# First loads, squares of the norm, and routing order in a fused attention and two-expert-layer kernel

## The chip, the cores and the metric
The kernel runs on one core of one Trainium2 chip. The core has five engines that each work through their own list of instructions in order: TensorE (PE, matrix products and transposes), VectorE (DVE), ScalarE (ACT), GpSimd (POOL) and SyncE (SP, which here only issues transfers). They wait for each other through semaphores. The metric is the device time of one launch in microseconds; it was 1309.68 us in the median of three runs (1309.29 to 1310.69).

## The reference
Three layers follow on each other for 4608 tokens (8 sequences of 576) of width 512:

```
kv  = einsum('bhsd,bhse->bhde', k, v)           # 8 heads of 64, no softmax
out = einsum('bhsd,bhde->bhse', q, kv)
x   = out / sqrt(mean(out*out, -1) + 1e-6) * g_norm
x   = (silu(x @ w_gate) * (x @ w_val)) @ w_out  # dense, hidden width 1536, weights float64
# routed: 8 experts of hidden width 1024, the best one per token
do  = x @ w_skip > 0                            # others pass unchanged
p   = softmax(x @ gate);  e = argmax(p)
y   = x + p[e] * (relu(x @ w1[e]) @ w2[e])      # where do
```

## The kernel before, in words
The work goes in 12 chunks of 384 tokens. The **attention** of a chunk has four units, one for each pair of heads (`attn_unit`). A unit multiplies k by v into a PSUM tile kvp (L211, only where a new sequence begins), copies its two diagonal blocks of 64 x 64 into kvbd, the first on ScalarE (L213), the second on VectorE (L214), multiplies the queries by kvbd into op (L227), squares op on ScalarE (sq, L233), adds the squares up head by head on VectorE (ms, L235), finishes the mean (L236), raises it to the power -1/2 on GpSimd (y, L238) and multiplies (xn, L240). `make_xT` transposes xn (xtps, L262) and splits it into a rounded part and the rest (L265, L266). Products in float32 are made from such pairs: each product is three matmuls.

The **gated layer** (MoE1) goes over 12 slices f of the hidden width in each chunk: gate and value products gv (L346), silu (L352), their product s (L353), the split into hT (L355 on ScalarE, L254 on GpSimd), and with a delay of one slice the accumulation acc (L367) in three PSUM banks. In chunk 0 the units of chunk 1 run between the slices; in later chunks those of the next chunk. Chunk 0 also turns the weights' 64-bit numbers into pairs: 18 transfers raw (L315, the last as two rawh, L324), and for each of 36 halves a rescale on ScalarE (L284), three bit operations on VectorE (L286, L287, L290), a rounding on ScalarE (L296) and the rest on GpSimd (L254). TensorE can begin a slice when its weights are converted.

The **routed layer** (MoE2) works with a list of tokens by expert. Each chunk's rows of x give nine logits a token, on VectorE (L400) during the next chunk, for the last chunk on TensorE (`logits_pe`: transposes ltp, L411, then matmuls lps, L416). `chunk_route` finds the expert and counts ranks by two small matmuls rp (L446, L447); then GpSimd scatters the rows (L454) into the memory xs, from which `load_xe` (L601) fetches a batch xe. A batch is transposed (xtp, L618) into xU, multiplied by the expert's first weights (hp, L633; hr, L655, in the batch of one tile) and its second (yacc, L721).

The first batch needs no rows of the last chunk. Its products hp and yacc fill TensorE while the last chunk is routed; the second batch needs the rows that this routing scatters.

The order within an engine is set by a scheduler that simulates the program ahead of time and takes what is ready first; `after(ins, to)` (L115) gives it an extra condition, which orders the list and adds no wait. SP's list holds all loads in one order: a load that waits for a buffer holds up those behind it. Tiles come from pools: wp has 18 buffers "w", p2 two of each name (kv, s for sq and s, ms), ps_acc three PSUM banks, ps_gv two, ps_x two, ps_c one.

Of the kernel before, what the change touches and what calls it, by code (L numbers as in the profile page):

```python
# [29 lines left out]
def attention_moe_moe_kernel(  # L30
# [98 lines left out]
    def attn_qt_load(c, pr):
        if c == 0:  # L130

            t = wp.tile([P, T], F32, tag="w", name="qt0")
        else:
            t = p1.tile([P, T + P], F32, tag="qt", name="qt")
# [204 lines left out]
    def moe1_g(c, f):  # L339
# [13 lines left out]
        nc.vector.tensor_tensor(s, ps[1], s, op=ALU.mult)  # L353
# [51 lines left out]
    def logits_pe(c, w9):  # L405
        lp = ps_acc.tile([P, R, P], F32, tag="acc", name="lps")
        for r in range(R):
            st = xrow[c, r]
# [6 lines left out]
            for kk in range(NK):  # L415
                nc.tensor.matmul(  # L416
# [7 lines left out]
    def chunk_route(c):  # L424
        lg = lgt.pop(c)
        wd = wdesc.rearrange("p (o e) -> p o e", o=1).to_broadcast([P, R, E])
        eb = (elast if c == NCH - 1 else ebase).rearrange("p (o e) -> p o e", o=1).to_broadcast([P, R, E])
# [592 lines left out]
```

## Time and profile before

| | |
|---|---|
| median of three runs | 1309.68 us |
| the profiled execution | 1305.69 us |
| its span (first to last instruction) | 1304.0 us |
| TensorE busy | 1266.1 us, 97% |
| VectorE, ScalarE, GpSimd busy | 639.3, 373.5, 510.6 us |
| chain that ended last | PE 85%, DVE 5%, DMA 4%, POOL 3% |
| mean granted TensorE clock | 0.995 |

The span is what the profile's times count; the profiled execution's own time stands beside it. Busy time over the whole span is a mean over stages: in one stage TensorE has no gap, in another it waits for a single load. A wait is named by the instruction that waited, the line, and what came last before it. Idle time of an engine that nobody waits for costs nothing. The granted clock is that of TensorE as a share of its upper level, 2.4 GHz.

### The profile page before, as it was taken

Reading aid. Unit: us, or ns where it says so; the run is one execution under the profiler, and the core shown is the slowest. Engines: PE = TensorE matmul, PEld = TensorE weight load, DVE = VectorE, ACT = ScalarE, POOL = GpSimd, SP = SyncE. Lnnn points to the kernel's source line nnn. Section 1 sums busy time; section 2 is a strip of 40 time slices with the busy share of each in tenths; the row PEclk is TensorE's granted clock in tenths of the full one; section 3 lists DMA queues with packets and bytes.
Section 4 is the critical chain, followed back from the end, with each engine's and each line's share of the span. In section 5 each row is a group of like instructions: output and inputs, shape, how many; then the busy total and the mean of one; then the engine's idle time right before and its main releaser. Section 6 shows DMA issues by size and latency. Waiting matters only on the chain.

```text
span 1304.0 us, 18975 instructions
## 1 busy us (share of the span) xinstructions
PE 1266.1 (97%) x7239; PEld 1180.2 (91%) x7239; DVE 639.3 (49%) x1487; ACT 373.5 (29%) x773; POOL 510.6 (39%) x545
## 2 busy tenths in 40 slices
PE   5998999999999999999999999999999989999997
PEld 5987999999999999999999999999988978899996
DVE  5896817237164371542815418146283243544662
ACT  3664112122121221211212112121122433344441
POOL 4674323233322332223323223223346443566662
PEclk9999999999999999999999999999999999999999
DMA  9663702021120111202102021110121343555631
GB/s 299 234 220 142 229 20 74 25 68 43 39 66 1 44 55 38 73 26 63 37 7 86 8 62 49 31 51 7 51 91 36 131 149 117 170 171 165 218 121 33
DMA packets 43205, 115.68 MB, mean 89 GB/s; under 512 B 8498, under 2 KB 16690, under 8 KB 40928
## 3 DMA queue, kind: packets, MB, share of 16 engines
q1 hardware_dynamic: 31888, 95.78, 22.7%
q0 software_dynamic: 6912, 9.82, 2.2%
q10 hardware_dynamic: 4304, 8.78, 2.1%
q8 instruction: 59, 0.97, 0.3%
q14 instruction: 42, 0.34, 0.1%
HBM read 88.70 MB, written 30.80 MB: 92 GB/s over the span
## 4 chain that ended last, share of the span: by engine, by line
PE 85%; DVE 5%; DMA 4%; POOL 3%; issue 2%; ACT 1%; SPq 0%; DVEq 0%; ACTq 0%; POOLq 0%
PE gv L346 42%; PE acc L367 21%; PE hp L633 7%; PE yacc L721 4%; PE tacc L687 3%; PE kvp L211 3%; PE op L227 2%; DVE dump L400 2%; PE xtps L262 1%; DMA kv<-in_kv_dram 1%; DMA xe<-xs_dram 1%; POOL v L254 1%; DMA raw<-in_w_dram 1%; DVE ex L585 1%; POOL w L254 1%
## 5 line engine op out<-in xcount | busy, mean ns | idle before, releaser
L346 PE MATMUL gv<-xT,w 128*128 128x384 f32 x3456 | 654.7, 339 | 3.8 <-ACT w L296 2.9
L346 PEld LDWEIGHTS gv<-xT,w 128*128 128x128 f32 x3456 | 602.1, 188 | 18.3 <-ACT w L296 4.2
L367 PE MATMUL acc<-w,hT 128*128 128x512 f32 x1296 | 333.3, 397 | 5.0 <-ACT hT L355 4.0
L254 POOL TENSOR_TENSOR hT<-s,hT 128x384 fp32r<-128x384 f32 x144 | 161.6, 1122 | 403.8 <-ACT hT L355 403.3
L367 PEld LDWEIGHTS acc<-w,hT 128*128 128x128 f32 x1296 | 239.3, 188 | 49.3 <-ACT hT L355 5.6
L400 DVE CUSTOM_DVE_ANT_0 dump<-st,w9b 128x512 bf16<-128x512 f32 x297 | 234.4, 789 | 7.0
L353 DVE TENSOR_TENSOR s<-gv,s 128x384 f32<-128x384 f32 x144 | 80.1, 556 | 253.0 <-PE gv L346 186.1
L254 POOL TENSOR_TENSOR v<-rawv,v 128x512 fp32r<-128x512 f32 x102 | 133.6, 1335 | 49.9 <-ACT v L567 49.7
L352 ACT ACTIVATE s<-gv 128x384 f32<-128x384 f32 x144 | 70.6, 490 | 260.4 <-PE gv L346 251.2
L355 ACT ACTIVATE hT<-s 128x384 fp32r<-128x384 f32 x144 | 75.5, 524 | 242.5 <-DVE s L353 241.1
L633 PE MATMUL hp<-xU,v 128*128 128x256 f32 (+7 forms) x768 | 125.8, 308 | 1.6 <-DVE xU L623 1.4
L633 PEld LDWEIGHTS hp<-xU,v 128*128 128x128 f32 x768 | 113.8, 189 | 4.7 <-DVE xU L623 1.7
L238 POOL TENSOR_TENSOR y<-ms,mhalf 128x6 f32<-128x6 f32 x48 | 68.2, 1422 | 109.7 <-DVE ms L236 107.8
L235 DVE TENSOR_REDUCE ms<-sq 128x6 f32<-128x384 f32 x48 | 26.4, 550 | 105.7 <-ACT sq L233 105.7
L567 ACT ACTIVATE v<-rawv 128x512 fp32r<-128x512 f32 x128 | 73.0, 623 | 1.9 <-DMA rawv<-in_v_dram 1.9
L721 PE MATMUL yacc<-v,h2T 128*128 128x512 f32 (+3 forms) x288 | 73.3, 397 | 0.0
L642 DVE SCALAR_TENSOR_TENSOR h2T<-hp,h2T 128x256 fp32r<-128x256 f32 (+7 forms) x64 | 30.5, 479 | 82.3 <-ACT h2T L641 81.1
L721 PEld LDWEIGHTS yacc<-v,h2T 128*128 128x128 f32 (+3 forms) x288 | 50.6, 181 | 11.2
L687 PE MATMUL tacc<-h2T,v 128*128 128x318 f32 (+3 forms) x384 | 58.1, 302 | 2.1 <-ACT h2T L641 2.1
L641 ACT ACTIVATE h2T<-hp 128x256 fp32r<-128x256 f32 (+7 forms) x64 | 27.2, 428 | 104.7 <-PE hp L633 92.1
L254 POOL TENSOR_TENSOR w<-raw,w 128x512 fp32r<-128x512 f32 x34 | 44.7, 1318 | 30.4 <-ACT w L296 29.5
L687 PEld LDWEIGHTS tacc<-h2T,v 128*128 128x128 f32 x384 | 53.8, 189 | 2.9 <-ACT h2T L641 2.8
(131 smaller groups left out, 875.8 us busy)
## 6 DMA issues: line engine op xcount, KB each, us to landing
rawv<-in_v_dram SPq DMA_DIRECT2D x64, 512.0 KB
kv<-in_kv_dram SPq DMA_DIRECT2D x32, 560.0 KB
raw<-in_w_dram SPq DMA_DIRECT2D x17, 1024.0 KB
out_dram<-st SPq DMA_DIRECT2D x36, 256.0 KB
xs_dram<-zrow ACTq DMA_DIRECT2D x8, 781.5 KB
qt<-in_qT_dram SPq DMA_DIRECT2D x32, 192.0 KB
qt<-in_qT_dram SPq DMA_DIRECT2D x32, 96.0 KB
w9b<-in_w_dram ACTq DMA_DIRECT2D x3, 768.0 KB
```

Of the source, the lines that this page charges most:

```text
L238: nc.gpsimd.tensor_tensor(y, ms, mhalf[:, 0:G], op=ALU.pow)
L254: return eng.tensor_tensor(lo, raw, hi.bitcast(F32), op=ALU.subtract)
L346: nc.tensor.matmul(pt, w1t[f][:, wi, i, kk, :], xT[c, kk][:, xi, :], start=(n == 0), stop=(n == 3 * NK - 1))
L352: step["silu"] = nc.scalar.activation(s, ps[0], AF.Silu)
L353: nc.vector.tensor_tensor(s, ps[1], s, op=ALU.mult)
L355: nc.scalar.activation(h[:, 0, :], s, AF.Copy)
L367: nc.tensor.matmul(acc[c, r], hT[c, f][:, hi, r * P:(r + 1) * P], w[:, wi, f % 2, :], start=(f == 0 and n == 0), stop=(f == NF - 1 and n = ...
L400: nc.vector.tensor_tensor_reduce(out=dump, in0=xrow[c, r][:, 0:DM], in1=w9b[m // 3][:, m % 3, :], op0=ALU.mult, op1=ALU.add, scale=1.0, sc ...
L567: after(nc.scalar.activation(w[:, 0, s], raw[:, s], AF.Copy), behind)
L633: nc.tensor.matmul(pt, w[:, wi, kk, cs], xT["m", b, kk][:, xi, :], start=(i == 0), stop=(i == 3 * NK - 1))
L687: nc.tensor.matmul(acc["m", b, d], w[:, wi, f % 2, d * P:(d + 1) * P], h[:, hi, :], start=(f == 0 and n == 0), stop=(f == NF2 - 1 and n == 2),
L721: ins = nc.tensor.matmul(acc["m", b, t][0:q], h[:, hi, t * q:(t + 1) * q], w[:, wi, f % 2, :], start=(f == 0 and n == 0), stop=(f == NF2 - ...
```

## The change
- Loads of k and v go over the flattened rows of the array, 128 rows in one transfer, where 116 were fetched in two (112 and 4). The rows past 116 are not used.
- Chunk 0: k, v and q of a pair share one buffer of wp (kvq). Three are asked for before the first unit. op of pairs 0 to 2 lies in the accumulators' banks, of pair 3 in a bank of gv.
- Chunks 0 and 1: ScalarE copies both blocks of kvbd, and six 64-wide squares that also add up their columns take the place of square and reduction.
- Chunk 1's loads of k, v and q are ordered behind the second weight's conversion. The first and second weights are asked for at other places.
- `chunk_route` ends with rp; the rest is `route_rows`, one slice later and behind s of that slice; `rank_experts` and `early_base` come another slice later.
- First routed batch: hp of slice 1 is ordered behind the second ltp, of slices 2 and 3 behind the last lps, later ones behind rp; yacc of slice 0 behind the last lps, later ones behind rp.

The core of the diff:

```diff
+    kv_rows = kv_d.rearrange("b q p s r c -> (b q p) s r c")
+    def attn_kv_load(c, pr, t, behind=None):
+        if c % 3 != 2:
+            b = 2 * (c // 3) + c % 3
+            row = (b * NPR + pr) * PK
+            n = min(P, B * NPR * PK - row)
+            for lo, hi in spread(n):
+                after(nc.sync.dma_start(t[lo:hi], kv_rows[row + lo:row + hi]), behind)
+            kvt[c, pr] = t
...
+    def attn_load_first(pr):
+        t = wp.tile([P, 2 * NR * P + T], F32, tag="w", name="kvq")
+        attn_kv_load(0, pr, t[:, 0:2 * NR * P].rearrange("p (s r c) -> p s r c", s=2, r=NR))
+        return t[:, 2 * NR * P:]
...
-        step["kv", c, pr] = nc.vector.tensor_copy(bd[D:P, D:P], kvp[D:P, D:P])
+        if c < 2:
+            nc.scalar.activation(bd[D:P, D:P], kvp[D:P, D:P], AF.Copy)
+        else:
+            nc.vector.tensor_copy(bd[D:P, D:P], kvp[D:P, D:P])
...
-            op = gv_tile([P, R, P], "op", True)
+            op = ps_acc.tile([P, R, P], F32, tag="acc", name="op") if pr < 3 else gv_tile([P, R, P], "op", True)
...
-        nc.scalar.activation(sq, opv, AF.Square)
-        nc.vector.tensor_reduce(ms, sq, axis=AX.X, op=ALU.add)
+        if c < 2:
+            for g in range(G):
+                nc.scalar.activation(sq[:, g, :], opv[:, g, :], AF.Square, accum_out=ms[:, g:g + 1])
+        else:
+            nc.scalar.activation(sq, opv, AF.Square)
+            nc.vector.tensor_reduce(ms, sq, axis=AX.X, op=ALU.add)
...
+        step["rp"] = nc.tensor.matmul(rp, onesb, ca[:, 0:R, :], start=False, stop=True)
+        chosen[c] = rp, oh, m1, mk
+    def route_rows(c, behind=None):
+        after(nc.vector.tensor_tensor(oh, rp, eb, op=ALU.add), behind)
...
-    attn_load(0, 1)
+    attn_qt_load(0, 1, attn_load_first(1))
+    qt2 = attn_load_first(2)
     attn_unit(0, 0)
-    for pr in range(1, NPR):
-        if pr + 1 < NPR:
-            attn_load(0, pr + 1)
-        attn_unit(0, pr)
+    attn_unit(0, 1)
     load_w1(0, (step["ms", 0, 0], step["ms", 0, 1]))
+    attn_qt_load(0, 2, qt2)
+    attn_qt_load(0, 3, attn_load_first(3))
+    attn_unit(0, 2)
+    attn_unit(0, 3)
...
-    load_w1(1)
+    load_w1(1, (step["ms", 0, 3], step["xn", 0, 3]))
...
-                    attn_load(c + 1, f // 3)
+                    attn_load(c + 1, f // 3, conv_done.get(1) if c == 0 else None)
...
-                if f == -(-(E + 1) * R // lpf):
+                f0 = -(-(E + 1) * R // lpf)
+                if f == f0:
                     chunk_route(c - 1)
+                if f == f0 + 1:
+                    route_rows(c - 1, step["gv"])
+                if f == f0 + 2:
                     if c == NCH - 2:
-                        rank_experts(c - 1)
+                        rank_experts(c - 1, step["gv"])
...
+    first_h = (None, step["ltp", 1], step["lps", R - 1], step["lps", R - 1], step["rp"])
+    first_y = (step["lps", R - 1], step["rp"])
...
-            moe2_h(b, f)
+            moe2_h(b, f, first_h[min(f, len(first_h) - 1)] if b == 0 else None)
...
-                        moe2_out(b, f - 1, t)
+                        moe2_out(b, f - 1, t, first_y[min(f, 2) - 1] if b == 0 else None)
```

What the lists hold at three places, before and now.

SP at the program's start, before (kv the k and v of a pair, qt0 its queries in chunk 0, qt those of chunk 1, raw a weight; the number is the buffer):
```order
L150 DMA kv_88<-in_kv_dram 112x1280
L150 DMA kv_88<-in_kv_dram 4x1280
L142 DMA qt0_91<-in_qT_dram 128x384
L150 DMA kv_166<-in_kv_dram 112x1280
L150 DMA kv_166<-in_kv_dram 4x1280
L142 DMA qt0_169<-in_qT_dram 128x384
L142 DMA qt0_195<-in_qT_dram 128x384
L142 DMA qt0_221<-in_qT_dram 128x384
L315 DMA raw_265<-in_w1_dram 128x2048
L139 DMA qt_377<-in_qT_dram 128x192
L140 DMA qt_377<-in_qT_dram 128x192
L150 DMA kv_192<-in_kv_dram 112x1280
```
SP there, now (kvq holds k, v and queries of a pair):
```order
L134 DMA kvq_88<-in_kv_dram 128x1280
L149 DMA kvq_88<-in_qT_dram 128x384
L134 DMA kvq_164<-in_kv_dram 128x1280
L149 DMA kvq_164<-in_qT_dram 128x384
L134 DMA kvq_167<-in_kv_dram 128x1280
L333 DMA raw_219<-in_w1_dram 128x2048
L149 DMA kvq_167<-in_qT_dram 128x384
L134 DMA kvq_233<-in_kv_dram 128x1280
L149 DMA kvq_233<-in_qT_dram 128x384
L333 DMA raw_318<-in_w1_dram 128x2048
```
The third pair's k and v moved in front of the first weight and have a buffer of their own; chunk 1's queries are gone from here.

ScalarE from the first unit on, before (kvbd: block copies, raw: rescale, w: rounded half of a weight):
```order
L213 ACTIVATE kvbd_93<-kvp 64x64
L213 ACTIVATE kvbd_97<-kvp 64x64
L233 ACTIVATE sq<-op 128x384 x2
L284 ACTIVATE raw<-raw 128x512 x2
L296 ACTIVATE w_0_267<-raw 128x512
L213 ACTIVATE kvbd_101<-kvp 64x64
L296 ACTIVATE w_0_267<-raw 128x512
```
ScalarE there, now:
```order
L222 ACTIVATE kvbd_91<-kvp 64x64
L224 ACTIVATE kvbd_91<-kvp 64x64
L222 ACTIVATE kvbd_95<-kvp 64x64
L224 ACTIVATE kvbd_95<-kvp 64x64
L250 ACTIVATE sq,ms<-op 128x64 x6
L222 ACTIVATE kvbd_99<-kvp 64x64
L224 ACTIVATE kvbd_99<-kvp 64x64
L250 ACTIVATE sq,ms<-op 128x64 x6
L302 ACTIVATE raw<-raw 128x512 x2
L250 ACTIVATE sq,ms<-op 128x64 x6
L314 ACTIVATE w_0_221<-raw 128x512
```
Twelve narrow squares stand in front of the first rescale of a weight, and eighteen in front of the first rounding.

TensorE where the last chunk is routed, before (two ltp x4 and 23 hp stand in front of these rows; v1 are the expert's first weights, v2 its second):
```order
L416 MATMUL lps_8870<-w9k_8845,lxt0_8876 128x128 x2
L416 MATMUL lps_8870<-w9k_8845,lxt1_8877 128x128 x2
L416 MATMUL lps_8870<-w9k_8845,lxt0_8889 128x128 x2
L416 MATMUL lps_8870<-w9k_8845,lxt1_8890 128x128 x2
L411 MATMUL ltp_8897<-ident_109,st_8866 128x128 x4
L721 MATMUL yacc0_9060<-v2_0_8264,h2T_9037 128x512 x3
L721 MATMUL yacc1_9064<-v2_0_8264,h2T_9037 128x512 x3
L721 MATMUL yacc0_9060<-v2_0_8264,h2T_9057 128x512 x3
L721 MATMUL yacc1_9064<-v2_0_8264,h2T_9057 128x512 x3
L633 MATMUL hp_9123<-xU3_8842,v1_2_8419 128x256
L416 MATMUL lps_8870<-w9k_8845,lxt0_8902 128x128 x2
L416 MATMUL lps_8870<-w9k_8845,lxt1_8903 128x128 x2
```
TensorE there, now:
```order
L429 MATMUL ltp_8881<-ident_107,st_8856 128x128 x4
L660 MATMUL hp_9041<-xU0_8821,v1_0_8210 128x256 x3
L660 MATMUL hp_9041<-xU1_8827,v1_0_8210 128x256 x3
L660 MATMUL hp_9041<-xU2_8833,v1_0_8210 128x256 x3
L660 MATMUL hp_9041<-xU3_8839,v1_0_8210 128x256 x3
L434 MATMUL lps_8867<-w9k_8842,lxt0_8873 128x128 x2
L434 MATMUL lps_8867<-w9k_8842,lxt1_8874 128x128 x2
L429 MATMUL ltp_8894<-ident_107,st_8863 128x128 x4
L434 MATMUL lps_8867<-w9k_8842,lxt0_8886 128x128 x2
L434 MATMUL lps_8867<-w9k_8842,lxt1_8887 128x128 x2
L434 MATMUL lps_8867<-w9k_8842,lxt0_8899 128x128 x2
L434 MATMUL lps_8867<-w9k_8842,lxt1_8900 128x128 x2
```
Between the first two ltp and the last lps 12 hp are left of 24 hp and 12 yacc; 6 yacc and 24 hp now stand between the last lps and rp.

## Rows read from the trace of the kernel before
**Rows 1.** Busy time by stretch: width, engines (instructions), granted clock, DMA share, GB/s
```profile
0.00:10.00 10.00, 3.52 (x15) 3.24 (x16) 0.68 (x3) 1.70 (x3) 3.55 (x45) 1.00 0.81 227
10.00:20.00 10.00, 7.58 (x34) 7.05 (x34) 5.96 (x14) 3.21 (x7) 4.00 (x3) 1.00 1.02 331
20.00:30.00 10.00, 4.86 (x30) 4.65 (x30) 8.83 (x18) 6.26 (x13) 6.03 (x5) 0.94 1.02 310
80.00:120.00 40.00, 34.41 (x170) 28.94 (x170) 31.75 (x51) 21.12 (x38) 25.83 (x21) 1.00 0.44 168
122.00:1025.00 903.00, 900.05 (x4999) 842.52 (x4998) 416.00 (x1096) 205.61 (x419) 296.71 (x319) 1.00 0.17 54
1061.00:1071.00 10.00, 9.06 (x57) 8.42 (x58) 5.23 (x18) 4.73 (x13) 5.22 (x6) 0.83 0.89 324
```

**Rows 2.** Waits of TensorE: for whom, us in total, times, longest
```profile
PE kvp L211 <- DMA kv<-in_kv_dram: 8.9, 4, 6.1
PE xtps L262 <- DVE xn L240: 5.1, 1, 5.1
PE acc L367 <- ACT hT L355: 4.0, 4, 1.6
...
PE xtp L618 <- DMA xe<-xs_dram: 2.8, 1, 2.8
...
PE acc L367 <- POOL hT L254: 1.1, 3, 0.4
...
PE xtp L618 <- DVE xU L623: 0.4, 1, 0.4
```

**Rows 3.** Timeline of TensorE, start: start us, us, instruction, idle before
```profile
16.21 2.47 PE L211 MATMUL kvp<-kv 116*128 116x128 f32 x10 [2.18 <-DMA kv<-in_kv_dram]
18.92 2.47 PE L211 MATMUL kvp<-kv 116*128 116x128 f32 x10 [0.24 <-DMA kv<-in_kv_dram]
...
28.89 0.88 PE L262 MATMUL xtps<-ident,xn 128*128 128x128 f32 x3 [5.14 <-DVE xn L240]
```

**Rows 4.** Tiles kvbd and sq by form: shortest, median, longest ns, first and last start
```profile
L213 ACT ACTIVATE kvbd<-kvp x32: 191/217/218, 8.7 to 859.5; 64x64 f32<-64x64 f32 x32
L214 DVE COPY kvbd<-kvp x32: 227/228/229, 8.9 to 859.8; 64x64 f32<-64x64 f32 x32
...
L233 ACT ACTIVATE sq<-op x48: 467/492/495, 12.8 to 940.2; 128x384 f32<-128x384 f32 x48
L235 DVE TENSOR_REDUCE ms<-sq x48: 541/553/553, 13.3 to 940.8; 128x6 f32<-128x384 f32 x48
```

**Rows 5.** VectorE to 122 us: one conversion step; its wait for squares
```profile
L287 DVE SCALAR_TENSOR_TENSOR cv<-raw,cv 128x512 int32<-128x512 int32 x34 | 23.6, 693 | 1.6
...
DVE ms L235 <- ACT sq L233: 4.9, 3, 2.7
```

**Rows 6.** Timeline of VectorE, end of the conversion
```profile
110.94 0.55 DVE L235 TENSOR_REDUCE ms<-sq 128x6 f32<-128x384 f32 x1 [2.71 <-ACT sq L233]
...
116.51 0.69 DVE L290 SCALAR_TENSOR_TENSOR rawh<-rawh,cv 128x512 int32<-128x512 int32 x1
```

**Rows 7.** Timeline of TensorE, the switch
```profile
1036.52 2.99 PE L633 MATMUL hp<-xU,v 128*128 128x256 f32 x23
...
1041.49 3.02 PE L721 MATMUL yacc<-v,h2T 128*128 128x512 f32 x12
...
1044.47 1.05 PE L416 MATMUL lps<-w9k,lxt 128*128 128x128 f32 x8
...
1051.34 0.19 PE L447 MATMUL rp<-cum,onesb 128*128 128x24 bf16 x1
...
1061.29 0.44 PE L618 MATMUL xtp<-ident,xe 128*128 128x128 f32 x2 [2.77 <-DMA xe<-xs_dram]
...
1065.21 3.67 PE L655 MATMUL hr<-v,xU 128*128 128x256 f32 x24
```

**Rows 8.** Timeline of GpSimd, the switch
```profile
1053.26 1.09 POOL L454 DMA_INDIRECT xs_dram<-st,idx  x1 [4.76 <-DVE cnf L842]
```

More of the change, by code (lines that the diff above doesn't have):

```diff
@@ L123, in after, with attn_qt_load @@
         return ins
+    kv_rows = kv_d.rearrange("b q p s r c -> (b q p) s r c")
[7 more added lines that the diff above has]
+            kvt[c, pr] = t
     def q_at(c, r):
         return r * P + (P if c % 3 == 1 and r > RS else 0)
[L129 to L134, printed above, removed]
+    def attn_qt_load(c, pr, t, behind=None):
         src = qT_d[pr, :, c * T:(c + 1) * T]
@@ L352, in moe1_g @@
         step["silu"] = nc.scalar.activation(s, ps[0], AF.Silu)
-        nc.vector.tensor_tensor(s, ps[1], s, op=ALU.mult)
+        step["gv"] = nc.vector.tensor_tensor(s, ps[1], s, op=ALU.mult)
         h = p2.tile([P, 2, T], F32R, tag="hT", name="hT")
@@ L415, in logits_pe @@
             for kk in range(NK):
-                nc.tensor.matmul(
+                step["lps", r] = nc.tensor.matmul(
                     lp[:, r, :], xt[kk // 2][:, kk % 2, :], w9[:, kk, :], start=(kk == 0), stop=(kk == NK - 1)
@@ L446, in chunk_route @@
         nc.tensor.matmul(rp, trib, mk, start=True, stop=False)
-        nc.tensor.matmul(rp, onesb, ca[:, 0:R, :], start=False, stop=True)
-        nc.vector.tensor_tensor(oh, rp, eb, op=ALU.add)
+        step["rp"] = nc.tensor.matmul(rp, onesb, ca[:, 0:R, :], start=False, stop=True)
+        chosen[c] = rp, oh, m1, mk
+    chosen = {}
+    def route_rows(c, behind=None):
+        rp, oh, m1, mk = chosen.pop(c)
+        eb = (elast if c == NCH - 1 else ebase).rearrange("p (o e) -> p o e", o=1).to_broadcast([P, R, E])
+        after(nc.vector.tensor_tensor(oh, rp, eb, op=ALU.add), behind)
         nc.vector.tensor_tensor(oh, oh, mk, op=ALU.mult)
@@ L480, in count, with by_rank @@
         return cp
-    def by_rank(src, name):
+    def by_rank(src, name, behind=None):
         t = xtp.tile([P, E, E], F32, tag="cmp", name="cmp")
-        nc.vector.tensor_tensor(t, sel, over(src, False), op=ALU.mult)
+        after(nc.vector.tensor_tensor(t, sel, over(src, False), op=ALU.mult), behind)
         o = p2.tile([P, E], F32, tag="rk" + name, name="rk" + name)
@@ L488, in by_rank, with rank_experts @@
         return o
-    def rank_experts(c):
+    def rank_experts(c, behind):
         key = p2.tile([P, E], F32, tag="key", name="key")
-        nc.vector.scalar_tensor_tensor(key, count(c), float(2 * E), wdesc, op0=ALU.mult, op1=ALU.add)
+        after(nc.vector.scalar_tensor_tensor(
+            key, count(c), float(2 * E), wdesc, op0=ALU.mult, op1=ALU.add
+        ), behind)
         t = xtp.tile([P, E, E], F32, tag="cmp", name="cmp")
@@ L512, in load_ranks, with early_base @@
             )
-    def early_base():
-        o = by_rank(count(NCH - 2), "o")
+    def early_base(behind):
+        o = by_rank(count(NCH - 2), "o", behind)
         nc.vector.tensor_scalar(adj, o[:, 0:1], -1.0, float(EARLY), op0=ALU.mult, op1=ALU.add)
@@ L623, in make_xT2, with moe2_h @@
         return nc.vector.tensor_tensor(xt[:, 1, :], tpf, xt[:, 0, :].bitcast(F32), op=ALU.subtract)
-    def moe2_h(b, f):
+    def moe2_h(b, f, behind=None):
         r, _, m, nt = BATCH[b]
@@ L632, in moe2_h @@
             for wi, xi in ((0, 0), (0, 1), (1, 0)):
-                nc.tensor.matmul(
+                ins = nc.tensor.matmul(
                     pt, w[:, wi, kk, cs], xT["m", b, kk][:, xi, :], start=(i == 0), stop=(i == 3 * NK - 1)
                 )
+                if i == 0:
+                    after(ins, behind)
                 i += 1
@@ L833, in attention_moe_moe_kernel @@
     chunk_route(NCH - 1)
+    route_rows(NCH - 1)
     load_xe(1)
```

23 lines of the change are left out of this document (9 added, 14 removed).

## The prediction
> **What bounds the kernel now.** I read the stretches of the span first [rows 1]. From 122 to 1025 us TensorE is busy for 900 of 903 us: eleven of the twelve chunks of the gated feed-forward network have no gaps, and nothing that the change moves there can pay. What TensorE loses lies before 122 us and near the end of the gated network. The waits of TensorE [rows 2] name the places: 8.9 us for four loads of k and v (6.1 of them the first load), 5.1 us for the normalised queries, 4.0 us for the hidden values hT, 2.8 us for the gathered tokens xe at the switch to the routed stage. Then I read three stretches instruction by instruction.
>
> The start. Up to 30 us TensorE is busy for 3.52, 7.58 and 4.86 of each 10 us [rows 1], and the loads run at 227, 331 and 310 GB/s, so the order of the loads decides when the units begin. The third unit's k and v arrive at 16.21 us, because their buffer is free only when the first unit has been read; the third unit's transposes wait 5.14 us until 28.89 us [rows 3].
>
> The rest of chunk 0. VectorE is busy for 8.83 of 10 us in the third stretch and 31.75 of 40 in the last [rows 1]. It converts 36 half weights with three operations of 0.69 us each [rows 5] = 74.5 us of the 102 us from the first half to the last one, which ends at 117.2 us [rows 6]. TensorE can't begin chunk 0's last slice before that half: it is busy for 34.41 of 40 us from 80 to 120 us [rows 1]. So chunk 0 ends when the conversion ends; a TensorE that starts earlier only waits longer for weights.
>
> The switch. The last chunk's router needs its rows transposed and multiplied (until 1045.5 us); then rank sums on TensorE (1051.34 us), the scatter, the load of the gathered rows, and at 1061.29 us the transposes that waited 2.77 us for it [rows 7, 8]. Right behind this the granted clock is 0.83 of the upper level [rows 1].
>
> **The change, part by part.** *Loads.* k and v come as one transfer of 128 rows, not 112 and 4: 32 issues less on SP, 10% more bytes. Where transfers have room (54 GB/s from 122 us on [rows 1]) this is nothing. At the start the bytes count: kv0, q0, kv1, q1, kv2 are 0.66 + 0.20 + 0.66 + 0.20 + 0.66 = 2.36 MB, and by the rates of rows 1 they are in at 10.3 us; I take 11, against 16.21. The first raw weight (3.4 MB in all) is in at 13.4 us, kv3 (4.3 MB) at about 16, against some 18.9.
>
> *Squares.* For eight units (chunks 0 and 1) one 384-wide square of 0.49 us and a reduction of 0.55 us on VectorE become six 64-wide squares on ScalarE that add up as they go, and a 0.23 us copy on VectorE becomes one of 0.22 on ScalarE [rows 4]. The trace has no square with a sum. From below, the 64-wide copy packs at about half of its 0.22 us, so six would take 0.7; from above, each costs what a whole 384-wide square does, 0.49, so six take 2.9 us. I take 0.25, near the copy of the same width: 1.5 us a unit. ScalarE then carries 1.5 - 0.49 + 0.22 = 1.2 us more a unit.
>
> That square of 0.49 us [rows 4] bears out a rule of the Trainium skill (ScalarE: Activation LUTs, "What ACT_TABLE_LOAD costs", whose last paragraph prices the ordinary instruction): a fixed 186 ns, 0.833 ns a column, 93 ns less where instructions follow on each other. By it six narrow squares take about 0.97 us against 0.51 for one wide, so it speaks against cutting the square up, yet gives 0.5 us a unit less than I do and would make the time about 1 us shorter. It gives no price for the sum; a second page (VectorE: DVE Perf Modes, "Two Vector instructions with no wait between them") says that on VectorE an operation that writes out its accumulator is two instructions. No row here shows either on ScalarE.
>
> What lies on the path: VectorE's conversion. From 15 us to the end VectorE is rid of two reductions of chunk 0, four of chunk 1 and six copies: 6 x 0.47 (0.55, less what overlaps with the next) + 6 x 0.2 = 4.0 us. Against this: ScalarE must rescale a weight before VectorE can convert it, and two units' squares (2 x 1.5, where 2 x 0.49 stood) now lie in front of the first rescale, so the first half starts some 2 us later. The second weight's arrival (5.5 MB, at about 20 us) takes most of that back, for VectorE waits there anyhow, and I reckon the two level by 45 us. Also VectorE now stops at the small operation ms where it stopped at the reduction, 4.9 us in three places, the longest 2.71 us at 110.94 us [rows 5, 6]; the squares end 1 us later each time, but the stop lies one 0.7 us conversion step later. About 0.3 x 3 is lost by it. Something comes from the earlier loads behind TensorE. Sum: 4.0 - 0.9 - 0.5 (what stays of the late start) + 1.4 (loads of weights that queue on SP behind loads waiting on TensorE, which is now some 5 us ahead) = 4.0 us earlier; between 0 and 8.
>
> *Earlier first slices.* With kv2 at 11 and kv3 at 16 us, and queries of three pairs in accumulator banks instead of two shared ones, the last transposes of the units come about 5 us earlier than the 29 to 32 us of today, by the two loads' gains of 5 and 3 us and by the 5.14 us idle time [rows 3], which goes. TensorE is ahead by that until it meets the conversion. This is not added to the 4.0: it is hidden behind it. It would be worth up to 5 more, and the 5.6 us idle of 80 to 120 us with it, if weights were ready.
>
> *Steady chunks.* The routing rows move by one slice, the ranking by one more. With 900.05 of 903 us busy I take 0; up to 2 us may come from it in chunk 11.
>
> *The switch.* Between the last accumulation and the last router matmul there stood 42 fillers hp and 12 yacc; now there are 18 hp. By rows 7, 23 hp take 2.99 us (0.13 each) and 12 yacc 3.02: 3.1 + 3.0 = 6.1 us less, from which I take 0.4 for the third row's multiplication that follows its transposes too closely. So the last router matmul ends at about 1039.8, not 1045.5. From there to the second rank sum it was 6.0 us; now 6 yacc and 24 hp stand between (1.5 + 3.1 = 4.6). The end at 1044.4 to 1045.8, scatter 1.75 us later, and 8.0 us from scatter to arrival as now [rows 8]: 1054.1 to 1055.6. TensorE was there at 1058.52 us; 12 yacc that were in front of the transposes now come behind them (3.0 us), so it gets there at 1055. The wait of 2.77 us shrinks to 0 or 0.6. With it go the short wait for xU behind it (0.4), the slower clock behind the idle time (24 hr in 3.67 us, where 0.13 each would be 3.1: 0.6), and some 0.6 of the 1.1 us that accumulations wait for hT from GpSimd [rows 2, 7], since fewer fillers stand in front of them. Sum 3.8 to 4.4; I take 4.4, bounds 0 (the arrival moves as the work does) and 7.
>
> **Sum.** The profiled execution took 1305.69 us (span 1304.0 and 1.7 around it); the timed runs lie 4 us above, at a median of 1309.68 us, and I keep this distance. 1305.69 - 4.0 - 4.4 = 1297.3, in the timed runs' terms 1301.3: **1301 us**. Own range with these bounds: 1296 to 1305.
>
> **Rivals.** A measurement of this kernel tells 0.2% from nothing, 2.6 us: faster is below 1307.1, slower above 1312.3.
>
> 1. *The start pays nothing.* Squares near 0.35 us each: the conversion's late start is not caught up and eats the 4.0. For it: ScalarE is in front of VectorE for every half weight. Against: ScalarE's gaps from 45 us on. Only the switch pays: 1309.7 - 4.4 = 1305.3.
> 2. *TensorE becomes the bound in chunk 0.* Weights keep ahead, and the start's 5 and the 5.6 idle us come out in full, 10.6, with the switch 15.0: 1294.7. Against it: 74.5 us of conversion don't get shorter.
> 3. *The switch moves its wait.* The scatter or the load of xe is late for another reason, or what is won waits at the next batch's operands (VectorE and xe again, 1081 us). Only the start pays: 1305.7.
> 4. *Slower: ScalarE becomes the bound of the conversion.* If a square with its sum costs as much as the wide square, 0.49, a unit takes 2.9 us of ScalarE, 2.4 + 0.2 more than now; for eight units 21 us, of which the four of the start stand in front of rescales and the four of chunk 1 in front of VectorE's ms. Loss 4 x (2.4 + 0.2) of the start, of which I let 2 be absorbed, = 8.4, less 4.0 of VectorE's work = 4.4, and 4 x 1 us in the ms stops: chunk 0 ends 8.4 us later; with the switch's 4.4 this is 1313.7. It decides from about 0.4 us a square on, where the loss passes the switch's gain.
> 5. *It does not do what it says.* kv2 still arrives near 16 us, as the 10% more bytes and the order of the transfers undo each other, and the switch is tied to GpSimd's splits of weights, not to TensorE's order: 1309.
>
> **How the numbers follow.** The forecast 0.42, rival 1 0.22, rival 2 0.10, rival 3 0.10, rival 4 0.08, rival 5 0.08. Faster: 0.42 + 0.20 + 0.10 + 0.06 = 0.78; slower: 0.08 and 0.01 = 0.09; same 0.13. For 8 in 10 the range must hold the forecast, rivals 1 and 3 and most of rival 2 and 5: 1293 to 1309; rival 4 and the tails, about 0.17, are left out.
>
> **What would show it.** Third unit's kvp at 11 us, not 16; last normalised queries before 25 us; six squares of a unit within 1.5 us; the last converted half at about 113 us (later than 117: the start failed; before 109: rival 2); rank sums at 1044 to 1046 us, no idle time above 0.6 us in front of the second batch's transposes, and a clock without the dip to 0.83 behind them. Wrong would be: squares of 0.4 us and more, or a new idle time of 2 us between 1025 and 1085 us.

## The result and the profile after

The changed kernel took 1295.09 us (median of 4, 1293.57 to 1297.01) against 1310.18 us: a ratio of 0.9883, 95% interval 0.9862 to 0.9904. Run again later it gave 0.9886 (0.9868 to 0.9905). So 15 us were won, where 8.4 were forecast; 1295 lies inside the range of 1293 to 1309. In the profiled executions the span fell from 1304.0 to 1292.0 us.

The stretches of the changed kernel that answer to [rows 1] (width, engines, granted clock, DMA share, GB/s; the last two bounds moved with the work):

```profile
0.00:10.00 10.00, 4.56 (x20) 4.43 (x21) 0.45 (x2) 1.92 (x4) 3.57 (x45) 1.00 0.77 276
10.00:20.00 10.00, 7.19 (x53) 6.37 (x51) 6.16 (x11) 7.16 (x46) 5.03 (x4) 1.00 1.02 421
20.00:30.00 10.00, 7.67 (x30) 6.09 (x30) 7.09 (x15) 6.78 (x23) 4.24 (x4) 0.83 0.79 321
80.00:120.00 40.00, 36.30 (x187) 31.30 (x187) 31.61 (x50) 23.27 (x61) 26.22 (x24) 1.00 0.43 160
122.00:1015.00 893.00, 891.08 (x4947) 833.97 (x4946) 413.00 (x1093) 200.55 (x410) 293.27 (x311) 1.00 0.17 55
1050.00:1061.00 11.00, 11.00 (x75) 9.91 (x74) 5.06 (x12) 5.67 (x15) 5.44 (x6) 1.00 0.42 159
```

Two rows speak at once. From 10 to 20 us the queues are as full as before (DMA share 1.02), yet carry 421 GB/s, not 331. And the stretch of the second routed batch, now 1050 to 1061 us, is full at a granted clock of 1.00, where it was 0.83.

TensorE's waits (answer to [rows 2]) and three places of its start (answer to [rows 3]):

```profile
PE kvp L220 <- DMA kvq<-in_kv_dram: 5.9, 2, 5.4
PE acc L385 <- ACT hT L373: 2.6, 4, 1.3
...
PE hp L660 <- DVE xU L650: 1.9, 1, 1.9
...
PE acc L385 <- POOL hT L272: 0.6, 2, 0.4
```

```profile
11.21 1.28 PE L220 MATMUL kvp<-kvq 116*128 116x128 f32 x10
...
14.53 1.35 PE L220 MATMUL kvp<-kvq 116*128 116x128 f32 x10 [0.46 <-DMA kvq<-in_kv_dram]
...
24.61 0.79 PE L280 MATMUL xtps<-ident,xn 128*128 128x128 f32 x3
```

The third pair runs at 11.21 us, not 16.21, the fourth at 14.53, not 18.92; the last transposes of xn stand at 24.61 us, and the 5.1 us wait for xn is gone.

ScalarE in the first unit's squares (answer to [rows 4]), and VectorE at the end of the conversion (answer to [rows 6]):

```profile
11.41 0.22 ACT L250 ACTIVATE sq<-op 128x64 f32<-128x64 f32 x1 [0.65 <-PE op L240]
11.53 0.19 ACT L250 ACTIVATION_READ_ACCUMULATOR sq<-op 128x1 f32 x1
11.62 0.22 ACT L250 ACTIVATE sq<-op 128x64 f32<-128x64 f32 x1
...
12.41 0.25 ACT L250 ACTIVATE sq<-op 128x64 f32<-128x64 f32 x1
12.52 0.24 ACT L250 ACTIVATION_READ_ACCUMULATOR sq<-op 128x1 f32 x1
```

```profile
106.52 0.17 DVE L254 TENSOR_SCALAR ms<-ms 128x6 f32<-128x6 f32 x1 [0.47 <-ACT sq L250]
...
111.47 0.69 DVE L308 SCALAR_TENSOR_TENSOR rawh<-rawh,cv 128x512 int32<-128x512 int32 x1
```

Each square is two instructions, the second one reading out the sum, and pairs follow at 0.20 us: 1.2 us a unit. The last converted half ends at 112.16 us, not 117.20, and the stop at ms is 0.47 us, not 2.71.

The switch (answer to [rows 7]), with the last products gv and the first router transposes in front of it:

```profile
1014.86 4.35 PE L364 MATMUL gv<-xT,w 128*128 128x384 f32 x24
...
1025.52 1.03 PE L429 MATMUL ltp<-ident,st 128*128 128x128 f32 x8
...
1029.16 1.95 PE L434 MATMUL lps<-w9k,lxt 128*128 128x128 f32 x16
...
1032.33 3.03 PE L660 MATMUL hp<-xU,v 128*128 128x256 f32 x24
...
1035.25 0.17 PE L465 MATMUL rp<-cum,onesb 128*128 128x24 bf16 x1
...
1048.13 0.38 PE L645 MATMUL xtp<-ident,xe 128*128 128x128 f32 x2
...
1052.84 3.24 PE L684 MATMUL hr<-v,xU 128*128 128x256 f32 x25
...
1070.62 1.22 PE L660 MATMUL hp<-xU,v 128*128 128x342 f32 x6 [1.90 <-DVE xU L650]
```

The last lps ends at 1031.1 us, rank sums follow at 1035.25, and the second batch's transposes at 1048.13 us wait for nothing; 25 hr take 3.24 us, where 24 took 3.67. The last line is a wait of 1.90 us that was 1.38 us at that place before. For comparison, the last gv and the first router transposes of the kernel before:

```profile
1021.05 4.35 PE L346 MATMUL gv<-xT,w 128*128 128x384 f32 x24
...
1035.73 1.03 PE L411 MATMUL ltp<-ident,st 128*128 128x128 f32 x8
```

Four landmarks of each profile, us from the span's start. A is the end of the last converted half, B the start of the first htp, TensorE's transposes of the second routed batch's hidden rows (1068.88 us before), then the span's end. Each row is one profiled execution; the first column has the starts of the third and fourth pair's kvp, the ratio is that of the timed runs to the kernel before, timed beside them.

| kernel | third, fourth pair | A | B - A | end - B | ratio |
|---|---|---|---|---|---|
| before | 16.2, 18.9 | 117.2 | 951.7 | 235.1 | 1 |
| changed | 11.2, 14.5 | 112.2 | 943.9 | 235.9 | 0.9883 |
| changed, again | 11.3, 14.5 | 113.0 | 944.6 | 238.1 | 0.9886 |
| without the order of the fillers | 11.7, 14.9 | 112.9 | 949.3 | 236.9 | 0.9943 |
| only the order of the fillers | 17.8, 20.6 | 119.3 | 948.0 | 237.7 | 0.9975 |
| without the split of the routing | 11.7, 14.9 | 112.6 | 947.0 | 236.3 | 0.9918 |
| wide squares | 11.7, 14.9 | 114.3 | 945.5 | 234.2 | 0.9916 |
| kv as 112 + 4 rows | 13.2, 19.3 | 115.6 | 945.9 | 235.4 | 0.9928 |
| kv as 112 + 16 rows | 13.3, 19.2 | 119.8 | 945.1 | 235.8 | 0.9932 |
| kv as 64 + 64 rows | 14.6, 19.6 | 121.3 | 945.6 | 237.3 | 0.9941 |
| before, kv as 128 rows | 13.9, 16.2 | 111.4 | 951.8 | 237.7 | 0.9927 |
| squares twice | 11.6, 14.8 | 126.5 | 947.5 | 236.3 | 0.9986 |
| later gate | 11.5, 14.9 | 113.7 | 945.2 | 234.3 | 0.9889 |
| xn on ScalarE, later gate | 11.4, 14.8 | 113.8 | 945.7 | 234.0 | 0.9885 |

The changed start gives A within 1.5 us (112.2 to 113.7, five profiles); the start of before gave 117.2 and 119.3. Eight profiles have both the order of the fillers and the split of the routing, without the doubled squares: their B - A lies between 943.9 and 945.9. The last column of times differs by 2.2 us between the two profiles of the changed kernel. Differences below these are not read from single profiles.

### The profile page after: what moved, and what is told of

The parts are those of the page before. It is cut to its first block, busy times and chain, and to the rows that moved or that the text cites. A ratio compares the mean times of both kernels' runs of the same rounds, so it can differ in the third digit from the quotient of the medians.

```text
span 1292.0 us, 19014 instructions
## 1 busy us (share of the span) xinstructions
PE 1262.5 (98%) x7239; PEld 1175.7 (91%) x7239; DVE 635.6 (49%) x1471; ACT 382.2 (30%) x869; POOL 512.6 (40%) x545
## 4 chain that ended last, share of the span: by engine, by line
PE 88%; DVE 4%; ACT 2%; DMA 2%; POOL 2%; issue 1%; SPq 0%; ACTq 0%; DVEq 0%; POOLq 0%
PE gv L364 43%; PE acc L385 21%; PE hp L660 8%; PE yacc L750 5%; PE tacc L716 3%; PE kvp L220 3%; PE op L240 3%; DVE dump L418 1%; PE xtps L280 1%; DMA raw<-in_w_dram 1%; POOL w L272 1%; DVE ex L612 1%; DMA xe<-xs_dram 1%; PE xtp L645 1%; ACT raw L302 0%
## 5 line engine op out<-in xcount | busy, mean ns | idle before, releaser
L660 PEld LDWEIGHTS hp<-xU,v 128*128 128x128 f32 x768 | 114.3, 189 | 5.0 <-DVE xU L650 2.2
L253 DVE TENSOR_REDUCE ms<-sq 128x6 f32<-128x384 f32 x40 | 22.0, 551 | 94.4 <-ACT sq L252 94.3
L750 PEld LDWEIGHTS yacc<-v,h2T 128*128 128x128 f32 (+3 forms) x288 | 50.3, 181 | 11.4 <-DVE h2T L671 0.4
L767 POOL DMA_INDIRECT out_dram<-y,ids x24 | 27.7, 1154 | 70.9 <-DVE y L764 50.8
```

The costliest lines, as they stand in the source:

```text
L660: ins = nc.tensor.matmul(pt, w[:, wi, kk, cs], xT["m", b, kk][:, xi, :], start=(i == 0), stop=(i == 3 * NK - 1))
L750: ins = nc.tensor.matmul(acc["m", b, t][0:q], h[:, hi, t * q:(t + 1) * q], w[:, wi, f % 2, :], start=(f == 0 and n == 0), stop=(f == NF2 - ...
```

## The experiments

**Without the order of the fillers.**

```diff
-            moe2_h(b, f, first_h[min(f, len(first_h) - 1)] if b == 0 else None)
+            moe2_h(b, f)
...
-                        moe2_out(b, f - 1, t, first_y[min(f, 2) - 1] if b == 0 else None)
+                        moe2_out(b, f - 1, t)
```

> The changed kernel without the two orders on the first routed batch (hp and yacc no longer behind ltp, lps and rp). Theory A (the fillers' place is what the switch gains by): the last lps comes some 6 us later against the last gated slice, the second batch's transposes wait 2 to 3 us again, the clock dips behind them; about 6 us are lost, ratio to the kernel before about 0.993. Rival B (the switch gains because GpSimd reaches hT earlier and the rows are routed in another order, not by the fillers): at most 1 us is lost, ratio 0.988 to 0.989.

Ratio 0.9943 (0.9921 to 0.9964); B - A grew by 4.7 to 5.4 us against the changed kernel's two profiles (3.4 to 5.4 against all eight with both edits). TensorE at the switch:

```profile
1044.77 0.19 PE L465 MATMUL rp<-cum,onesb 128*128 128x24 bf16 x1
...
1054.79 0.44 PE L645 MATMUL xtp<-ident,xe 128*128 128x128 f32 x2 [2.85 <-DMA xe<-xs_dram]
```

The second rank sum comes 10.0 us before transposes that wait 2.85 us, as before the change. Theory A holds.

**Only the order of the fillers**, in the kernel before (the same lines, added).

> The kernel before with nothing but the two orders on the first routed batch. Theory A: everything up to 1025 us stays, the wait of 2.77 us for the gathered rows goes, 5 to 6.5 us are won from 1025 to 1070 us, ratio 0.995 to 0.996. Rival B: the wait stays at 2 us or more and no more than 2 us are won, ratio 0.998 to 1.000.

Ratio 0.9975 (0.9962 to 0.9988), B - A 3.7 us shorter: the wait is gone, but less is won than the 5 to 6.5 us of theory A. Part of what is missing is found below, where the routing is put back in one piece.

**Wide squares.**

```diff
-        if c < 2:      # at both places: block copy, and squares with their sums
+        if False:
```

> The changed kernel with one wide square and the reduction on VectorE, and the second block copy on VectorE, in chunks 0 and 1 as before. Theory C (chunk 0 ends earlier because VectorE is rid of reductions and copies): the last converted half comes 4 us later, at about 116 us instead of 112.2, and chunk 0's last gv at about 116; the ratio goes from 0.988 to 0.991. Rival D (it ends earlier because the loads come earlier and in another order): the last half stays within 1.5 us of 112.2 us.

A came at 114.3 us in this one profile: 0.6 to 2.1 us later than the five of the changed start, less than the 4 of theory C. The ratio, 0.9916 (0.9901 to 0.9931), lies 0.003 above the changed kernel's 0.9883 and 0.9886, which is some 4 us, with intervals that overlap at their ends. Both point to a relief of VectorE that is worth something; between 0.6 and 4 us its size is not settled.

**k and v in two transfers, 112 and 4 rows.**

```diff
-            n = min(P, B * NPR * PK - row)
+            n = PK
```

> The changed kernel with k and v loaded as 112 and 4 rows (10% fewer bytes, one transfer more a pair). Theory C: the third and fourth pair arrive up to 2 us later, chunk 0 still ends with the conversion, so the last gv of chunk 0 moves by less than 1 us. Rival D: 10 to 20 us runs at 331 GB/s as before instead of 421, raw weights come 2 us later, and chunk 0 ends 1.5 to 3 us later.

Ratio 0.9928 (0.9910 to 0.9946). TensorE's fourth pair, then the transfers from 5 to 20 us, then for comparison the changed kernel's from 5 to 10 us:

```profile
19.34 1.97 PE L220 MATMUL kvp<-kvq 116*128 116x128 f32 x10 [1.46 <-DMA kvq<-in_kv_dram]
```

```profile
5.00:10.00 5.00, 2.80 (x11) 2.57 (x12) 0.00 (x0) 0.43 (x2) 0.00 (x0) 1.00 1.03 266
10.00:15.00 5.00, 5.00 (x32) 4.98 (x31) 0.17 (x1) 2.07 (x16) 0.03 (x1) 1.00 1.03 319
15.00:20.00 5.00, 1.74 (x13) 1.43 (x12) 3.89 (x9) 4.34 (x27) 2.72 (x3) 0.99 1.01 309
```

```profile
5.00:10.00 5.00, 4.56 (x20) 4.43 (x21) 0.00 (x0) 0.44 (x2) 0.00 (x0) 1.00 1.03 404
```

With 10% fewer bytes of k and v and the same full queues (DMA share 1.01 to 1.03) the rate is 266 to 319 GB/s, where the changed kernel has 404 to 423. The fourth pair is 4.8 us later and A 2 to 3.5 us. Rival D is right here, and theory C, by which the end of chunk 0 would move by less than 1 us, is wrong.

**112 and 16 rows; 64 and 64 rows.**

```diff
-            for lo, hi in spread(n):
+            for lo, hi in ((0, 112), (112, n)) if n == P else spread(n):   # in the second run (0, 64), (64, n)
```

> The changed kernel with each pair's 128 rows of k and v in two transfers of 112 and 16 rows: the bytes of the change, the number of transfers of before. In the changed kernel a 5 KB packet took 225 ns up to 22 us and the transfers ran at 404 to 423 GB/s, with 112 and 4 rows 316 ns and 266 to 319 GB/s. Theory F (the piece of 4 rows slows the others down): packets stay near 225 ns, the fourth pair arrives by 15.5 us, chunk 0 ends as in the changed kernel within 1 us. Rival G (one more transfer a pair, or 112 rows in one, slows them): packets near 300 ns, fourth pair at 17 to 19 us, chunk 0 ends 2 to 4 us later.

> The changed kernel with each pair's 128 rows of k and v in two transfers of 64 rows. Theory L (a transfer of 112 rows is what slows the queue: it shared the time in both slow forms, 112 and 4, 112 and 16): 5 KB packets stay near 235 ns, the fourth pair arrives by 15.5 us, chunk 0's last half at 112 to 114 us. Rival M (two transfers for one are what slows it): packets at 300 ns or more, the fourth pair at 17 to 19.5 us, last half at 115 us or later.

Ratios 0.9932 (0.9916 to 0.9949) and 0.9941 (0.9922 to 0.9959), A at 119.8 and 121.3 us. One stretch of the transfers of the form 112 and 16, then those of the form 64 and 64:

```profile
10.00:15.00 5.00, 5.00 (x24) 5.00 (x25) 0.05 (x1) 1.78 (x14) 0.00 (x0) 1.00 1.01 322
```

```profile
5.00:10.00 5.00, 2.48 (x10) 2.21 (x10) 0.00 (x0) 0.44 (x2) 0.00 (x0) 1.00 1.06 257
10.00:15.00 5.00, 4.83 (x26) 4.87 (x27) 0.00 (x0) 1.48 (x13) 0.00 (x0) 1.00 0.98 308
15.00:20.00 5.00, 2.13 (x17) 1.81 (x16) 3.60 (x9) 4.90 (x32) 2.90 (x3) 1.00 1.06 307
```

All the bytes of the changed kernel, full queues, and 257 to 308 GB/s. It is neither the piece of 4 rows (F) nor the 112 (L): in all three cuts two transfers for a pair are slow, and one is fast (rivals G and M). By the packet times in the traces from 5 to 20 us, a 5 KB packet of k and v takes 199 to 205 ns in the mean with one transfer (nine profiles) and 287 to 335 ns with two (five), an 8 KB packet of the weights 311 to 313 and 344 to 402 ns: k and v's own packets lose most. The number of transfers alone is not a likely cause, since from 20 to 25 us, when only weights arrive, each in a transfer of its own over 128 rows, the kernel with 112 and 4 rows runs at 420 GB/s. What the three cuts have in common is also that no transfer of k and v reaches over all 128 rows of the buffer. No run has two transfers for a pair that both do, so what costs the rate stays open.

**The kernel before, with k and v as 128 rows in one transfer and nothing else.**

```diff
-            for lo, hi in spread(PK):
-                nc.sync.dma_start(t[lo:hi], kv_d[b, pr, lo:hi])
+            row = (b * NPR + pr) * PK
+            n = min(P, B * NPR * PK - row)
+            for lo, hi in spread(n):
+                nc.sync.dma_start(t[lo:hi], kv_d.rearrange("b q p s r c -> (b q p) s r c")[row + lo:row + hi])
```

> The kernel before with one edit: k and v as 128 rows in one transfer. If the rate of the transfers is worth what the two slower forms cost in the changed kernel: packets of 5 KB fall from 290 to 225-240 ns, the third pair still waits for its buffer but arrives 2 to 4 us earlier than 16.2 us, chunk 0 ends 2 to 3 us earlier, ratio 0.9975 to 0.9985. Rival (in the old order the conversion hides it): under 1 us, ratio 0.999 to 1.001.

Ratio 0.9927 (0.9913 to 0.9941), three to five times the gain expected. Its transfers, its end of the conversion, and VectorE's wait for squares:

```profile
5.00:10.00 5.00, 4.61 (x20) 4.47 (x21) 0.23 (x1) 0.22 (x1) 0.00 (x0) 1.00 1.03 404
10.00:15.00 5.00, 2.86 (x19) 2.67 (x18) 3.59 (x9) 2.33 (x5) 2.61 (x2) 0.87 1.03 419
15.00:20.00 5.00, 4.59 (x32) 4.35 (x32) 3.88 (x9) 2.67 (x6) 2.39 (x3) 0.79 1.00 418
```

```profile
110.70 0.69 DVE L292 SCALAR_TENSOR_TENSOR rawh<-rawh,cv 128x512 int32<-128x512 int32 x1
```

```profile
DVE ms L237 <- ACT sq L235: 0.4, 1, 0.4
```

A is at 111.39 us, before that of any kernel with the change's whole start. The wait for squares, 4.9 us in [rows 5], is 0.4 us here though squares and reductions are those of before. ScalarE's waits from 15 to 120 us show what went, the kernel before first, then this one:

```profile
ACT raw L284 <- DMA raw<-in_w_dram: 14.6, 7, 3.1
...
ACT rawh L284 <- DMA rawh<-in_w_dram: 2.5, 1, 2.5
```

```profile
ACT raw L286 <- DMA raw<-in_w_dram: 8.3, 7, 2.1
```

ScalarE stood 17.1 us before weights that had not arrived; whatever came after in its list (hT, then by way of GpSimd the buffer of the next square) stood with it. In the kernel before, these two rows of ScalarE stand in front of VectorE's longest stop, that of 2.71 us up to 110.94 us:

```profile
108.21 0.67 ACT L284 ACTIVATE rawh<-rawh 128x512 f32<-128x512 f32 x1 [2.53 <-DMA rawh<-in_w_dram]
...
110.41 0.49 ACT L233 ACTIVATE sq<-op 128x384 f32<-128x384 f32 x1 [0.20 <-POOL hT L254]
```

With the faster transfers 8.3 of the 17.1 us are left. The second profile of the old start, in the kernel with only the order of the fillers, agrees with the first: 17.2 us before weights, and 4.5 us of waiting for squares.

**The routing of a chunk in one piece.**

```diff
                 if f == f0:
                     chunk_route(c - 1)
-                if f == f0 + 1:
-                    route_rows(c - 1, step["gv"])
+                    route_rows(c - 1)
```

(`rank_experts` and `early_base` likewise)

> The changed kernel with the routing of a chunk in one piece again (scatter rows and ranking in the slice of the rank sums). Theory H (the split is what frees GpSimd before the switch and 1 us of chunk 11's stalls): chunk 11's stalls go from 2.7 back to 4 us, the first router transposes come 12.5 us after the last gated slice's start, not 10.7, and about 2 to 3 us are lost in all. Rival I (the split is worth nothing): less than 0.7 us is lost.

Ratio 0.9918 (0.9894 to 0.9942), B - A 2.4 to 3.1 us longer than in the changed kernel's two profiles. GpSimd in front of the switch, here and in the changed kernel:

```profile
1013.16 10.01 POOL L272 TENSOR_TENSOR v<-rawv,v 128x512 fp32r<-128x512 f32 x8
1023.12 2.00 POOL L272 TENSOR_TENSOR hT<-s,hT 128x384 fp32r<-128x384 f32 x2
```

```profile
1017.44 5.07 POOL L272 TENSOR_TENSOR v<-rawv,v 128x512 fp32r<-128x512 f32 x4
1022.43 1.05 POOL L272 TENSOR_TENSOR hT<-s,hT 128x384 fp32r<-128x384 f32 x1
```

In one piece eight splits of weights run in a row, 10.0 us, with two hT behind them, as before the change; split, hT comes after four. The kernel with only the fillers' order has the eight in a row, too. B - A by stretches, each from the end of the one before, in us (last gv, last lps: their ends; the others: their starts; xtp: the second batch's):

| kernel | A to last gv | first ltp | last lps | second rp | xtp | B |
|---|---|---|---|---|---|---|
| before | 908.2 | 10.3 | 9.8 | 5.8 | 9.9 | 7.6 |
| only the order of the fillers | 908.2 | 8.5 | 5.6 | 4.1 | 12.9 | 8.7 |
| without the order of the fillers | 907.1 | 9.2 | 9.8 | 5.8 | 10.0 | 7.4 |
| without the split of the routing | 908.3 | 7.4 | 5.6 | 4.1 | 12.9 | 8.7 |
| changed | 907.0 | 6.3 | 5.6 | 4.1 | 12.9 | 7.9 |

The split takes 1.1 us out of the stretch in front of the first router transposes, with the fillers' order and without it, and some 1.2 us of stalls before the last gv. Theory H's mechanism is seen; its 2 to 3 us are reached in these profiles, but not in all. Ten profiles have the split. Six of them have 906.8 to 907.1 us from A to the last gv, the other four (wide squares, 112 + 4 rows, later gate, xn on ScalarE) 908.1 to 909.1, and in exactly these four the granted clock was below 1.00 between 960 and 1000 us, behind the stall of 1.3 us in chunk 11. There the 1.2 us are lost again.

**Squares twice.**

```diff
             for g in range(G):
+                nc.scalar.activation(sq[:, g, :], opv[:, g, :], AF.Square, accum_out=ms[:, g:g + 1])
                 nc.scalar.activation(sq[:, g, :], opv[:, g, :], AF.Square, accum_out=ms[:, g:g + 1])
```

> The changed kernel with each narrow square done twice, the first result overwritten: 1.2 us more of ScalarE a unit by the measured spacing of 0.2 us (2.4 in place of 1.2), as my dearest square. Theory J (ScalarE has room; only the squares in front of the first rescales count): chunk 0 ends 1 to 2.5 us later than in the changed kernel. Rival K (ScalarE bounds the conversion at that price): chunk 0 ends 5 to 10 us later, all that the start gained is lost.

A went to 126.5 us, 13 to 14 us later; ratio 0.9986 (0.9973 to 0.9999), some 13 us above the changed kernel's. That is rival K, beyond its 5 to 10 us. VectorE's waits for squares:

```profile
DVE ms L255 <- ACT sq L251: 17.3, 5, 13.7
DVE s L372 <- ACT sq L250: 5.7, 1, 5.7
```

The 13.7 us are not one stop in the middle: they begin at 3.6 us, before any k and v are there, and end with the first ms at 17.32 us. In the changed kernel this wait is 9.2 us and ends at 12.79, so VectorE's conversion starts 4.5 us later. Up to 98.19 us it stood another 5.7 us in front of s, behind squares in ScalarE's list. In this profile the granted clock was also lower than in the changed kernel's (0.60 against 0.91 from 20 to 40 us, 0.83 against 1.00 from 80 to 100 us), so how the 13 to 14 us divide is not shown; that 9.6 us more of ScalarE's work cost more than their own length is.

**Later gate.** The gate of the next routed batch, a softmax that begins on VectorE, is ordered behind the current batch's xU.

```diff
-        nc.vector.tensor_reduce(m[0:q], lg, axis=AX.X, op=ALU.max)
+        after(nc.vector.tensor_reduce(m[0:q], lg, axis=AX.X, op=ALU.max), behind)   # behind the batch's xU
```

> The changed kernel with the gate of the next routed batch ordered on VectorE behind the current batch's operands xU. In the changed kernel the third large batch's gate waited 5.0 us for its load, with two xU behind it, and TensorE waited 1.9 us for those at 1070 us. Theory: that wait goes, 1.5 to 1.9 us are won in all. Rival: the same load is waited for by the next transposes, nothing is won.

From 1060 to 1100 us, the changed kernel and this one:

```profile
1060.00:1100.00 40.00, 38.10 (x213) 33.35 (x212) 14.89 (x27) 14.85 (x33) 16.36 (x14) 1.00 0.41 130
```

```profile
1060.00:1100.00 40.00, 39.72 (x222) 34.74 (x221) 16.64 (x29) 17.53 (x39) 18.80 (x16) 1.00 0.43 136
```

TensorE is busy for 1.6 us more of the stretch, and its wait of 1.90 us for xU is gone from its list of waits. But end - B is only 1.6 us shorter, less than is read here, and the time, ratio 0.9889 (0.9869 to 0.9908), can't tell the two kernels apart.

**The changed kernel again, and xn on ScalarE** (the second with the later gate, and in chunk 1 only):

```diff
-        step["xn", c, pr] = nc.vector.tensor_tensor(
...
+        if c == 1:
+            for g in range(G):
+                step["xn", c, pr] = nc.scalar.activation(xtv[:, g, :], opv[:, g, :], AF.Copy, scale=y[:, g:g + 1])
...
```

> The changed kernel once more, for the comparison with the three beside it: ratio 0.986 to 0.990, chunk 0's last converted half at 111.5 to 113.5 us, since unchanged code gave 112.2 to 113.7 so far.

> The changed kernel with the later gate (which took away 1.9 us of waiting at the third large batch) and with chunk 1's normalising product as six 64-wide scaled copies on ScalarE, not one product of 0.55 us on VectorE. Theory (VectorE bounds the conversion, ScalarE still has room): chunk 0's last half comes 1.5 to 2 us earlier, 110 to 111 us, and with the gate 3 us are won, ratio 0.986. Rival (ScalarE is by now as tight, as the doubled squares showed): the half comes at 112 us or later, ratio 0.988 or more.

The changed kernel came out as expected (0.9886, A at 113.0 us). With xn on ScalarE A is at 113.8 us, ratio 0.9885 (0.9862 to 0.9907): the rival. Less work on VectorE at ScalarE's expense brings A no earlier, and the move wins nothing. No version here is told apart from the changed kernel as faster. One that was not tried is the start of before with k and v as one transfer (A at 111.4), with the fillers' order and the split; whether it would be faster is open.

## Why the forecast came out as it did

**Sign and place: right.** The steady chunks gave little (1.9 us idle of 893, where it was 2.95 of 903), the gain lies before A and at the switch, and the kernel is faster. The size, 15 us for 8.4, was not foreseen.

**The loads: the step that failed.** The prediction costed one transfer for two at "nothing" in the steady state and, at the start, by its bytes at the rates of [rows 1], so as 10% dearer. But those rates are the rates of split transfers: in full queues, by stretches of 5 us from 5 to 20 us, 236 to 354 GB/s with two a pair (five kernels), 394 to 424 with one (nine profiles). This edit alone won 0.73% and brought A to 111.4 us, 5.8 to 8.0 us earlier than the two profiles of the old start. The arrivals that the prediction drew from the old rates (third pair 11, fourth 16 us) came out as 11.2 and 14.5.

The Trainium skill (DMA: Bandwidth & Descriptors, "Rules for kernel authors") advises against two transfers to disjoint halves of the partitions and for one of 128, since both halves share the same engines. The runs agree: the form with two halves ran at 257 to 308 GB/s where the changed kernel ran at 404 to 423, 26 to 36% less.

**VectorE's relief: right in kind, its size not settled.** 4.0 us were forecast. Taking it away again put A 0.6 to 2.1 us later in one profile, and the time some 4 us higher with intervals that overlap. That the sum of 4.0 for the start came near the 5.0 measured is luck: the one transfer, which was costed at no gain, brings A earlier by more than that alone. The 1.4 us in that sum for weights queuing behind TensorE were not measured by any run. The stops at ms, taken as the squares' own (with "0.3 x 3" lost), were for the most part late weights in disguise: they went from 4.9 and 4.5 us to 0.4 us in the kernel that kept the old squares. The other edits of the start (early k and v in buffers of their own, accumulators' banks, order behind conversions) bring TensorE's first gv from 26.9 us, with the one transfer alone, to 18.8 us, and, as forecast, that is hidden. A is 0.8 to 2.3 us later with all of them than with the one transfer alone; that is one profile against five, and no more than the 2.1 us between the two profiles of the old start, so it is not shown that any of them costs time.

**Squares: within the bounds.** 0.20 us each, 1.2 a unit, against 1.5 taken and bounds of 0.7 and 2.9. By the Trainium skill (ScalarE: Activation LUTs, "What ACT_TABLE_LOAD costs") a narrow square is estimated at 239 ns, a fixed 186 ns and 0.833 ns for each of 64 columns. The trace agrees: 0.22 to 0.25 us in the rows shown. The six come to 1.2 us and not to the 0.97 that the prediction worked out from the same figures, as the read-out of the sum is an instruction of its own here. Rival 4 needed 0.4 us a square: at 2.4 us a unit A came at 126.5 us, 9.3 later than before, where the rival had 8.4. That dear squares make chunk 0 end later is shown; the price was not the case, and the nearness of 9.3 to 8.4 is partly luck, as that kernel also has the faster loads, which the rival did not reckon with.

**The switch: right in mechanism, too small.** 4.4 us were forecast, 7.1 to 7.8 measured in B - A in the changed kernel's two profiles (5.8 to 7.8 in all eight with both edits). The rank sums came 9.7 us after the first router transposes, not 15.6, and the wait of 2.77 us, the one for xU behind it and the dip of the clock all went, as worked out. From the last acc to the last lps it is 6.1 us, not 11.8, which is the 5.7 us of the prediction. What its sum lacks lies in front of that: from the last gv to the last acc it is 5.8 us, not 8.4, with 6 hp between them where there were 18, and an earlier hT from GpSimd. Mis-sized were the 0 for the steady chunks, with its "up to 2 us", and "some 0.6" for GpSimd: the split of the routing, which was costed there, gave 2.4 to 3.1 us where the clock held, 1.1 of it in front of the switch, where GpSimd's order had changed, which was not looked at. The order of the fillers gave 3.7 us alone and 4.7 to 5.4 with the split.

**Given back: 0.5 us** at the third large batch, where a gate waits for the load of its rows with two xU behind it.

**Profile against time.** The forecast was drawn from one execution. Its start was an early one: the same start gave A at 117.2 and 119.3 us, and the profiled execution lay 4.5 us below the median of 1310.18, that of the changed kernel 1.3 below its own. So 12.0 us of gain between two profiled executions are 15 between medians, and 3 of the 6.7 us by which the forecast fell short are this.

## What to carry to other kernels

A rate read from a full queue belongs to the form of the transfers in it; when a change alters the form, the rate is an unknown and has to be bounded from both sides like any other price. When an engine's list stops at a small instruction, follow the wait back through the lists it crosses: here VectorE waited for squares, these for a buffer, this for hT, and that stood behind a weight that had not landed. A term that comes out right may have another cause, and only undoing the parts one at a time shows it.

## What the runs showed that was not expected

- Two transfers for a pair's k and v (rows of 5 KB) in place of one cut the rate of the full queues from 394 to 424 GB/s to 257 to 322, in three ways to cut (112 + 4, 112 + 16, 64 + 64), all in the changed kernel from 5 to 20 us.
- A square that adds up its columns is a pair of instructions on ScalarE, 0.20 and 0.19 us at the shortest, 0.23 and 0.22 us in the median, 0.20 us from pair to pair.
- Doubling squares of 1.2 us a unit, 9.6 us of ScalarE in all, made chunk 0's last half come 13 to 14 us later.
- A stall of 1.3 us in chunk 11, in front of acc, is in all profiles with the split; from 960 to 980 us the granted clock was 1.00 in the changed kernel and 0.93 in the one with the later gate, whose edit lies behind it, and the matmuls of acc followed each other at 0.43 us, not 0.23. That is 1.5 us between two executions with the same order up to there.
